# Attention feeding a maxout layer: the values' bound by one product with ones, and feed-forward products dealt out to beats by time

## The chip, the cores and the metric

The kernel runs on one core of one Trainium2 chip. The metric is the time of one execution on the device in microseconds (us); lower is better. A time is the median of several runs; a profile is one execution of its own, with a time of its own.

## The reference

Attention over 8 batches, 12 heads, 448 positions and 64 numbers a head, with queries and keys normalized first; its output, 3584 tokens of 768 numbers, goes through three 768 by 768 products whose elementwise maximum goes through a fourth. All inputs and the output are float32.

```
q_n, k_n = rmsnorm(q, g_q), rmsnorm(k, g_k)       # x / sqrt(mean(x*x) + 1e-6) * g
scores = matmul(q_n, k_n.T) / sqrt(64)
attn = exp(scores - max(scores)); attn = attn / (sum(attn) + 1e-9)
x = matmul(attn, v)                               # then [batch * seq, heads * dim]
h = maximum(maximum(x @ w1, x @ w2), x @ w3)
out = h @ w_out
```

## The kernel before, in words

**Precision.** A float32 operand is held as two float16 parts, an upper one and the rest, and a product is made of three float16 products (`TERMS`). So that the parts fit, operands are scaled by their largest magnitude. For the values of a batch that bound is made by `bound_v` (line 489) with `largest` (line 145): the largest of each partition is turned into one row by a product with the identity (`marks`, line 153), reduced on VectorE to one number (`top`, line 156), and spread to all partitions by a product with a row of ones (`most`, line 160). From it come `v_down` and `v_up` (lines 494 and 498). The bounds of the weights are made in the same way, through the same `largest`.

**The unit of attention** is a pair of heads `g`, 48 in all, six to a batch. The 448 queries of a pair are worked in four quarters, here called chunks. For a chunk, TensorE makes the scores (`sc`, line 541, 6 products), VectorE finds the row maxima (line 550), ScalarE takes the exponentials in place (`nm` line 558, line 567), VectorE the inverse of the sums (lines 636 and 640), ScalarE writes the upper half of the weights (`pp`, line 643), VectorE the lower half (line 653), and a transposing DMA turns them into `pt`. When all four are turned, TensorE multiplies them with the values (`av`, line 691, 24 products), and `xt` (lines 705 and 706) is one sixth of the feed-forward input of the batch. The first six pairs go another way (`PLAIN`), in float32. There are two buffers of scores: the scores of chunk k+1 go into the buffer of chunk k-1, and so wait for line 653 of chunk k-1.

**The unit of the feed-forward** is a generator that issues, at every step, three products; six steps make a block. `layer1` (line 715) makes a 128 by 448 block with 6 steps of three products of 448 columns; three blocks make one maximum (`hidden`, line 727). `layer2` (line 775) makes a 128 by 384 block of the output with 6 steps of three products of 384 columns; `result` (line 791) copies it scaled on ScalarE into `osb` (line 793), and `store` writes it out. A batch has 18 blocks of `layer1` (324 products) and 6 or, for odd batches, 8 blocks of `layer2` (108 or 144). All these blocks, and `marks` and `most`, take turns in three PSUM buffers (`ps_m`, tag "m").

**The order** is written by hand: each engine runs its instructions in the order in which the kernel issues them. A pair takes 12 beats (`beat(g, i)`, line 904). In a beat stand the attention steps due there (scores in beats 2, 5, 8 and 11, the values' product in beat 7), then `thirds(THIRDS[i])` steps of the feed-forward queue, then the works put off by `later(n, work)`, which are issued n beats later, at the end of that beat, by `tick`. `THIRDS` adds up to 25 steps a pair; one more is taken in beats 4 and 10 while two batches stand in the queue. A batch is put in the queue when its last pair is done, in beat 10 (beat 6 for the first). What is left of the last batch runs after the last pair, two steps a beat.

The chain of a step that ends a block: the next call of the generator puts the work that reads the block (`hidden` or `result`) off by one beat.

Of the kernel before, what the change touches and what calls it, by code (L numbers as in the profile page):

```python
# [9 lines left out]
F32 = mybir.dt.float32  # L10
# [6 lines left out]
P = 128  # L17
# [10 lines left out]
UP = 2.0 ** 14  # L28

LEAST = 2.0 ** -60  # L30
# [9 lines left out]
def qknorm_attention_maxout_ffn_kernel(  # L40
# [35 lines left out]
    nc = tc.nc  # L76
    B, H, S, D = q.shape
# [9 lines left out]
    HW = DO // NH  # L87
# [5 lines left out]
    const = ctx.enter_context(tc.tile_pool(name="const", bufs=1))  # L93
# [3 lines left out]
    ps_m = ctx.enter_context(tc.tile_pool(name="ps_m", bufs=3, space=bass.MemoryType.PSUM))  # L97
# [15 lines left out]
    def later(beats, work, last=False):  # L113

        due.setdefault(clock[0] + beats, ([], []))[last].append(work)
# [10 lines left out]
    make_identity(nc, ident)  # L126
    ones = const.tile([1, P], F32, name="ones")
    nc.vector.memset(ones, 1.0)
    warm = const.tile([P, 1], F32, name="warm")
    nc.vector.memset(warm, 0.0)  # L130
    nc.scalar.activation(warm, warm, AF.Exp)
# [13 lines left out]
    def largest(column, done, gaps):  # L145


        top = sb.tile([1, 1], F32, name="top", bufs=2)
        box = []

        def turn():
            box.append(ps_m.tile([P, 512], F32, name="marks", tag="m"))
            nc.tensor.matmul(box[0][0:1, 0:P], column, ident, start=True, stop=True)

        def reduce():
            nc.vector.tensor_reduce(top, box[0][0:1, 0:P], axis=AX, op=ALU.max)

        def spread():
            box.append(ps_m.tile([P, 512], F32, name="most", tag="m"))
            nc.tensor.matmul(box[1][:, 0:1], ones, top, start=True, stop=True)  # L160

        at = 0
        for gap, work in zip(gaps, (turn, reduce, spread, lambda: done(box[1][:, 0:1]))):
            at += gap
            later(at, work)
# [182 lines left out]
    def load_k(g):  # L348
        load_kv(g, "kr", k, 2, (nc.sync, nc.sync if g else nc.scalar))
# [130 lines left out]
    v_down = const.tile([P, B], F32, name="v_down")  # L480
# [8 lines left out]
    def bound_v(b):  # L489
        most = sb.tile([P, 1], F32, name="v_most", bufs=2)  # L490
        nc.vector.tensor_reduce(most, v_rows.pop(b), axis=AX, op=ALU.max)

        def scale(bound):
            nc.vector.tensor_scalar(
                out=v_down[:, b:b + 1], in0=bound, scalar1=LEAST, scalar2=1.0 / UP,
                op0=ALU.max, op1=ALU.mult,
            )
            nc.vector.reciprocal(v_up[:, b:b + 1], v_down[:, b:b + 1])

        largest(most, scale, (1, 2, 2, 2))  # L500


    def scale_v(g):
# [166 lines left out]
    def add_values(g):  # L670
        s = st[g]
        av = ps_a.tile([P, 512], F32, name="av", tag="a")
        s["av"] = av
        if g < PLAIN:
            vr, pt = s["vr"], pt_plain(s)
            for u in range(4):
                for h, half in enumerate(HALVES):
                    rows = half if u == 3 else slice(0, P)
                    group = 3 if u == 3 else 4 * h + u
                    nc.tensor.matmul(  # L680
                        av[half, :S], vr[rows, group], pt[rows, group],
                        start=u == 0, stop=u == 3,
                    )
            return
        vp, pt = s["vp"], s["pt"]
        for u in range(4):
            for n, (wp, vpart) in enumerate(TERMS):
                for h, half in enumerate(HALVES):
                    rows = half if u == 3 else slice(0, P)
                    group = 3 if u == 3 else 4 * h + u  # L690
                    nc.tensor.matmul(  # L691
                        av[half, :S], vp[rows, group, vpart], pt[rows, 7 * wp + group],
                        start=u == 0 and n == 0, stop=u == 3 and n == len(TERMS) - 1,
                    )
# [20 lines left out]
    def layer1(b, xs, hs, ft, j, keep):  # L715
        wt = w_sb[:, ft * NJ + j].rearrange("p a (c f) -> p a c f", c=NCT)
        acc = ps_m.tile([P, 512], F32, name="acc", tag="m")
        for c in range(NCT):
            for n, (wp, xp) in enumerate(TERMS):
                nc.tensor.matmul(  # L720
                    acc[:, :S], wt[:, wp, c], xs[c][:, xp],
                    start=(c == 0 and n == 0), stop=(c == NCT - 1 and n == 2),
                )
            yield
        later(1, lambda: hidden(b, acc, hs, ft, j, keep))

    def hidden(b, acc, hs, ft, j, keep):
        if j == 0:
            keep[ft] = sb.tile([P, S], F32, name="m", bufs=2)
            nc.scalar.copy(keep[ft], acc[:, :S])  # L730
            return
        m = keep[ft]
        most = m if j == 1 else acc[:, :S]
        nc.vector.tensor_tensor(out=most, in0=acc[:, :S], in1=m, op=ALU.max)
        if j == 2:
            ht = sb.tile([P, 2, S], F16, name="ht", bufs=6)
            hs.append(ht)

            def upper():
                nc.scalar.activation(ht[:, 0], most, AF.Copy, scale=H_DOWN)  # L740
                later(1, lower)

            def lower():
                nc.vector.scalar_tensor_tensor(  # L744
                    out=ht[:, 1], in0=most, scalar=H_DOWN, in1=ht[:, 0],
                    op0=ALU.mult, op1=ALU.subtract,
                )
                odd = (b % 2) * LEFT
                nc.gpsimd.tensor_copy(hx[:, ft, :, odd:odd + LEFT], ht[:, :, 3 * P:S])  # L749

            later(1, upper)


    def store(b, osb, row0, col0, n):
        tok = out[b * S:(b + 1) * S].rearrange("(p c) m -> c p m", c=NQ)
        while n:
            c, p0 = divmod(col0, QP)
            m = min(n, QP - p0)
            nc.sync.dma_start(out=tok[c, p0:p0 + m], in_=osb[row0:row0 + m])
            row0, col0, n = row0 + m, col0 + m, n - m  # L760
# [14 lines left out]
    def layer2(b, hs, tk, half, box):  # L775
        if half == 0:
            box[tk] = sb.tile([P, DO], F32, name="osb", tag="osb", bufs=3)
        osb = box[tk]
        acc = ps_m.tile([P, 512], F32, name="acc", tag="m")
        for f in range(NFT):  # L780
            assert f in split
            for n, (hp, wp) in enumerate(TERMS):
                lhs = hs[f][:, hp, tk * P:(tk + 1) * P] if tk < 3 else hx[:, f, hp]
                nc.tensor.matmul(  # L784
                    acc[:, :HW], lhs, wo_sb[:, f, wp, half * HW:(half + 1) * HW],
                    start=(f == 0 and n == 0), stop=(f == NFT - 1 and n == 2),
                )
            yield
        later(1, lambda: result(b, acc, osb, tk, half))

    def result(b, acc, osb, tk, half):
        by = o_scale[:, b:b + 1] if tk < 3 else o_pair[:, b // 2:b // 2 + 1]
        nc.scalar.activation(  # L793
            osb[:, half * HW:(half + 1) * HW], acc[:, :HW], AF.Copy, scale=by
        )
        if half == NH - 1:
            if tk < 3:
                later(2, lambda: store(b, osb, 0, tk * P, P))
            else:
                later(2, lambda: store(b - 1, osb, 0, 3 * P, LEFT))  # L800
                later(2, lambda: store(b, osb, LEFT, 3 * P, LEFT))
# [23 lines left out]
    queue = []  # L825
    decoded = [0]

    def thirds(n):
        while queue and n:
            try:  # L830
                next(queue[0])
                n -= 1
            except StopIteration:
                queue.pop(0)

    load_k(0)
    load_q(0)
# [2 lines left out]
    for i, src in enumerate((g_q, g_k)):  # L840
        nc.scalar.dma_start(
            out=gains[:, i], in_=src.rearrange("(o d) -> o d", o=1).broadcast_to([P, D])
# [53 lines left out]
    load_q(2)  # L896


    THIRDS = (2, 3, 2, 2, 3, 2, 2, 0, 2, 2, 3, 2)

# [1 line left out]
    def beat(g, i):  # L904
# [36 lines left out]
        if w >= 0 and i == (4 if w < PLAIN else 7):  # L941
            add_values(w)
        thirds(THIRDS[i] + (len(queue) > 1 and i % 6 == 4))
        if w >= 0 and i == (9 if w < PLAIN else 10):
            finish(w, x_of[w // NP])
# [35 lines left out]
        if g == 0 and i == 9:  # L981
            bound_v(0)
        if g > 1 and g % NP == 0 and g < G and i == 1:
            bound_v(g // NP)
# [28 lines left out]
    while queue or due:  # L1013
        thirds(2)
        tick()
# [32 lines left out]
```

## Time and profile before

| | |
|---|---|
| median of 3 runs | 1111.87 us (1109.64 to 1112.04) |
| the profiled execution, its own time | 1110.84 us |
| its span, first to last instruction | 1109.0 us |
| mean granted TensorE clock | 0.967 |
| busy: TensorE, ScalarE, VectorE, GpSimd | 92%, 70%, 68%, 63% of the span |
| first feed-forward product | 162.48 us |
| last product of attention (line 691) begins | 1013.33 us |

In the profile PE is TensorE's products, PEld its weight loads, DVE VectorE, ACT ScalarE, POOL GpSimd. A row of the timeline gives start, duration, engine, line, operation, output and inputs with their shapes, the count, and in brackets how long the engine sat idle before it and whom it waited for. The duration of a product is modelled and longer than its share of a dense row of products: what a product costs in such a row is read from the starts of what comes before and after, or from the chain, whose pieces do not overlap. A row of the waits gives who waited for whom, the sum, how often, and the longest.

### The profile page before, as it was taken

The numbers are of one execution on the slowest core, as the hardware profiler recorded it, in microseconds if no ns is written. First come the engines' busy times: TensorE is split into PE (matmuls) and PEld (weight loads), VectorE is DVE, ScalarE is ACT, GpSimd is POOL, SyncE is SP. The second block draws the span as 40 slices with busy tenths as digits, with TensorE's granted clock in tenths as the row PEclk, the third lists the DMA queues.
The fourth block names the chain that finished last, engine by engine and source line by source line (L and its number), as shares of the span: only waits on it lengthen the run. The fifth ranks groups of instructions, "written<-read, shape, count | busy, mean of one in ns | idle before, by whom it ended". The sixth has DMA issues, their size and how long they took to land. (4 is left out here: it accounts for less than half of the span.)

```text
span 1109.0 us, 18435 instructions
## 1 busy us (share of the span) xinstructions
PE 1017.1 (92%) x6184; PEld 500.3 (45%) x6184; DVE 755.3 (68%) x1397; ACT 771.2 (70%) x1767; POOL 702.4 (63%) x805
## 2 busy tenths in 40 slices
PE   4668759887899999999999999999999999999998
PEld 2334334343444444444444444444444444445554
DVE  4799988887667676776677766777677666662210
ACT  4599888767777687777777777777777777773001
POOL 5478888775767767677677675776767767610000
PEclk9697879998999999999999999999999999999999
DMA  5554567955888779777887798777877788564002
GB/s 150 161 164 151 139 175 142 188 118 102 172 147 147 134 153 179 152 142 139 170 149 143 143 164 173 144 137 154 169 142 139 140 173 154 91 106 87 1 1 57
DMA packets 426494, 152.30 MB, mean 137 GB/s; under 512 B 372896, under 2 KB 422048, under 8 KB 426400
## 3 DMA queue, kind: packets, MB, share of 16 engines
q1 hardware_dynamic: 425888, 150.95, 67.4%
q8 instruction: 49, 0.80, 0.3%
q14 instruction: 45, 0.37, 0.1%
q10 hardware_dynamic: 512, 0.18, 0.1%
HBM read 51.97 MB, written 11.01 MB: 57 GB/s over the span
## 5 line engine op out<-in xcount | busy, mean ns | idle before, releaser
L720 PE MATMUL acc<-xt,w_sb 128*128 128x448 f16 x2592 | 515.5, 354 | 2.7 <-DVE ht L744 2.2
L720 PEld LDWEIGHTS <-w_sb 128*128 128x128 f16 x2592 | 244.1, 98 | 260.8 <-issue 48.3
L550 DVE TENSOR_REDUCE sc<-sc 112x2 f32<-112x896 f32 x192 | 209.6, 1092 | 53.3 <-PE sc L541 52.2
L567 ACT ACTIVATE sc<-sc,nm,down 112x448 f32<-112x448 f32 x336 | 234.4, 698 | 11.2
L643 ACT ACTIVATE pp<-sc,rs 112x448 f16<-112x448 f32 x336 | 195.0, 633 | 52.0 <-ACT sc L567 47.4
L653 DVE SCALAR_TENSOR_TENSOR pp<-sc,rs,pp 112x448 f16<-112x448 f32 x336 | 212.9, 675 | 4.4 <-ACT pp L643 3.9
L784 PE MATMUL acc<-wo_sb,ht 128*128 128x384 f16 x864 | 151.9, 328 | 12.0 <-ACT osb L793 7.3
L558 ACT ACTIVATE nm<-sc,down 112x2 f32<-112x2 f32 x192 | 50.9, 265 | 158.2 <-DVE sc L550 157.7
L385 POOL TENSOR_TENSOR ri<-ri,half_neg 128x7 f32<-128x7 f32 x96 | 153.9, 1603 | 8.0
L541 PE MATMUL sc<-kt,qt 64*112 64x448 f16 x1008 | 132.1, 367 | 21.5 <-DVE pp L653 18.6
L749 POOL COPY hx<-ht 128x128 f16<-128x128 f16 x48 | 16.2, 337 | 168.0 <-DVE ht L744 167.6
L784 PEld LDWEIGHTS <-ht 128*128 128x128 f16 x864 | 81.4, 98 | 79.4 <-issue 29.0
L691 PE MATMUL av<-pt,vp 128*64 128x448 f16 x1008 | 109.9, 359 | 0.0
L541 PEld LDWEIGHTS <-qt 64*112 64x112 f16 x1008 | 54.2, 126 | 91.6 <-issue 52.4
L438 POOL TENSOR_TENSOR kp<-kn,kp 128x512 f16<-128x512 f32 x42 | 50.5, 1202 | 67.1 <-ACT kp L432 67.1
L636 DVE TENSOR_SCALAR rs<-sc 112x2 f32<-112x2 f32 x168 | 26.7, 159 | 91.1 <-ACT sc L567 91.0
L519 POOL TENSOR_TENSOR vp<-vr,vp 128x448 f16<-128x448 f32 x42 | 44.5, 1059 | 63.0 <-ACT vp L513 61.3
L691 PEld LDWEIGHTS <-vp 128*64 128x64 f16 x1008 | 50.1, 109 | 54.7 <-issue 29.5
L706 DVE SCALAR_TENSOR_TENSOR xt<-av,xt 128x448 f16<-128x448 f32 x42 | 26.2, 625 | 67.0 <-ACT xt L705 67.0
L370 DVE TENSOR_REDUCE ss<-sq 128x7 f32<-128x448 f32 x96 | 61.0, 637 | 10.4 <-ACT sq L361 6.4
L438 POOL TENSOR_TENSOR qp<-qn,qp 112x512 f16<-112x512 f32 x42 | 48.6, 1156 | 19.2 <-ACT qp L432 19.2
L505 POOL TENSOR_SCALAR vr<-vr,v_up 128x448 f32<-128x448 f32 x42 | 60.4, 1438 | 0.0
(111 smaller groups left out, 1202.6 us busy)
## 6 DMA issues: line engine op xcount, KB each, us to landing
raw<-in_moe_w_dram SPq DMA_DIRECT2D x18, 768.0 KB, 4.3
qr<-in_q_dram SPq DMA_DIRECT2D x48, 224.0 KB, 2.8
vr<-in_v_dram SPq DMA_DIRECT2D x96, 96.0 KB, 2.5
kr<-in_k_dram SPq DMA_DIRECT2D x95, 96.0 KB, 3.0
raw<-in_moe_w_out_dram SPq DMA_DIRECT2D x6, 768.0 KB, 5.1
pt<-pp SPq DMA_TRANSPOSE x168, 4.0
out_dram<-osb SPq DMA_DIRECT2D x8, 336.0 KB, 3.0
out_dram<-osb SPq DMA_DIRECT2D x8, 288.0 KB, 3.6
```

Of the source, the lines that this page charges most:

```text
L370: nc.vector.tensor_reduce(sums[g % 2][:sq.shape[0], KQ[what]], sq, axis=AX, op=ALU.add)
L385: nc.gpsimd.tensor_tensor(out=ri, in0=ri, in1=half_neg[:, at], op=ALU.pow)
L438: nc.gpsimd.tensor_tensor(out=parts[:, 1], in0=n, in1=parts[:, 0], op=ALU.subtract)
L505: nc.gpsimd.tensor_scalar(out=vr, in0=vr, scalar1=v_up[:, g // NP:g // NP + 1], scalar2=None, op0=ALU.mult,)
L541: nc.tensor.matmul(sc[:QP, h, :S], qt[rows, qp, c], kt[rows, kp, KEYS[h]], start=n == 0, stop=n == len(TERMS) - 1,)
L550: nc.vector.tensor_reduce(sc[:QP, 0, S + 8:S + 10], sc[:QP, :, :S], axis=AX, op=ALU.max, negate=True)
L567: nc.scalar.activation(to, sc[:QP, h, :S], AF.Exp, bias=nm[:, h:h + 1], scale=down[:QP], accum_out=total,)
L643: nc.scalar.activation(pp[:, 0, h], sc[:QP, h, :S], AF.Copy, scale=rs[:, h:h + 1])
L653: nc.vector.scalar_tensor_tensor(out=pp[:, 1, h], in0=sc[:QP, h, :S], scalar=rs[:, h:h + 1], in1=pp[:, 0, h], op0=ALU.mult, op1=ALU.subtract,)
L691: nc.tensor.matmul(av[half, :S], vp[rows, group, vpart], pt[rows, 7 * wp + group], start=u == 0 and n == 0, stop=u == 3 and n == len(TERMS ...
L720: nc.tensor.matmul(acc[:, :S], wt[:, wp, c], xs[c][:, xp], start=(c == 0 and n == 0), stop=(c == NCT - 1 and n == 2),)
L784: nc.tensor.matmul(acc[:, :HW], lhs, wo_sb[:, f, wp, half * HW:(half + 1) * HW], start=(f == 0 and n == 0), stop=(f == NFT - 1 and n == 2),)
```

## The change

Four edits:

1. `bound_v` no longer calls `largest`. It makes one product of a 128 by 128 matrix of ones (one column of ones, read again and again) with the column of the partitions' largest (`spread`, put off by two beats), so that every partition gets their sum. That sum stands in place of the largest as the bound; `v_down` and `v_up` follow one beat later. The bounds of the weights stay as they were.
2. A step of `layer1` counts 1.0 and a step of `layer2` counts 384/448, and `thirds` keeps what is owed from beat to beat: it issues steps while half a step or more is owed.
3. `THIRDS` has a 2 where it had its second 3 (beat 4), so that a pair is given 24.
4. `result` is put off by no beat: it is issued in the beat in which the next step finds the block ended.

```
+    ones_c = const.tile([P, 1], F32, name="ones_c")
+    nc.vector.memset(ones_c, 1.0)
...
-        def scale(bound):
+        box = []
+
+
+        def spread():
+            box.append(ps_m.tile([P, 512], F32, name="most", tag="m"))
+            nc.tensor.matmul(
+                box[0][:, 0:1], ones_c.broadcast_to([P, P]), most, start=True, stop=True
+            )
+
+        def scale():
             nc.vector.tensor_scalar(
-                out=v_down[:, b:b + 1], in0=bound, scalar1=LEAST, scalar2=1.0 / UP,
+                out=v_down[:, b:b + 1], in0=box[0][:, 0:1], scalar1=LEAST, scalar2=1.0 / UP,
                 op0=ALU.max, op1=ALU.mult,
             )
             nc.vector.reciprocal(v_up[:, b:b + 1], v_down[:, b:b + 1])
 
-        largest(most, scale, (1, 2, 2, 2))
+        later(2, spread)
+        later(3, scale)
...
-            yield
+            yield 1.0
         later(1, lambda: hidden(b, acc, hs, ft, j, keep))
...
-            yield
-        later(1, lambda: result(b, acc, osb, tk, half))
+            yield HW / S
+        later(0, lambda: result(b, acc, osb, tk, half))
...
+    owed = [0.0]
+
     def thirds(n):
-        while queue and n:
+        owed[0] += n
+        while queue and owed[0] >= 0.5:
             try:
-                next(queue[0])
-                n -= 1
+                owed[0] -= next(queue[0])
             except StopIteration:
                 queue.pop(0)
+        if not queue:
+            owed[0] = 0.0
...
-    THIRDS = (2, 3, 2, 2, 3, 2, 2, 0, 2, 2, 3, 2)
+    THIRDS = (2, 3, 2, 2, 2, 2, 2, 0, 2, 2, 3, 2)
```

What this moves, read from the order of the built programs. On PE, in the second layer of batch 1, where the bound of batch 3 is made, there stood before (`acc` are the blocks, `ht` the second layer's input, `vp` the values):

```order
L784 MATMUL acc_4372<-wo_sb_95,ht_3444 128x384
L153 MATMUL marks_4382<-ident_72,v_most_4359 1x128
L784 LDWEIGHTS ht_3629
...
L784 MATMUL acc_4413<-wo_sb_95,ht_3956 128x384
L160 MATMUL most_4462<-top_4361,ones_77 128x1
L691 LDWEIGHTS vp_4312
```

and now:

```order
L796 MATMUL acc_4371<-wo_sb_97,ht_3613 128x384
L500 MATMUL most_4384<-v_most_4343,ones_c_79 128x1
L796 LDWEIGHTS ht_3819
...
L796 MATMUL acc_4413<-wo_sb_97,ht_3819 128x384
L703 LDWEIGHTS vp_4292
```

One product and one PSUM buffer are left of two, at about the place of the first; the second, ahead of the values' product, is gone.

On ACT, in the second layer of batch 2, from the exponentials of chunk 0 of a pair (`sc_5799`) to the upper half of chunk 1, there stood before:

```order
L567 ACTIVATE sc_5799<-sc_5799,nm_5819,down_128 112x448 x2
L432 CAST kp_5831<-kn1_89 128x512
L793 ACTIVATE osb_5673<-acc_5674,o_scale_103 128x384
L793 ACTIVATE osb_5673<-acc_5753,o_scale_103 128x384
L643 ACTIVATE pp_5846<-sc_5799,rs_5843 112x448 x2
L432 CAST qp_5858<-qn_5777 112x512
L558 ACTIVATE nm_5887<-sc_5865,down_128 112x2
L567 ACTIVATE sc_5865<-sc_5865,nm_5887,down_128 112x448 x2
L793 ACTIVATE osb_5809<-acc_5810,o_scale_103 128x384
L643 ACTIVATE pp_5906<-sc_5865,rs_5903 112x448 x2
```

and now:

```order
L579 ACTIVATE sc_5774<-sc_5774,nm_5794,down_130 112x448 x2
L434 CAST kp_5811<-kn1_91 128x512
L805 ACTIVATE osb_5719<-acc_5720,o_scale_105 128x384
L805 ACTIVATE osb_5719<-acc_5761,o_scale_105 128x384
L655 ACTIVATE pp_5826<-sc_5774,rs_5823 112x448 x2
L434 CAST qp_5838<-qn_5745 112x512
L570 ACTIVATE nm_5863<-sc_5844,down_130 112x2
L579 ACTIVATE sc_5844<-sc_5844,nm_5863,down_130 112x448 x2
L805 ACTIVATE osb_5806<-acc_5807,o_scale_105 128x384
L655 ACTIVATE pp_5888<-sc_5844,rs_5885 112x448 x2
```

These copies stand where they stood: the second layer of this batch begins later by some products, and its copies follow their blocks sooner by a beat. The last copy of the same batch moves. Before, from the exponentials of the pair's last chunk on:

```order
L643 ACTIVATE pp_6044<-sc_6000,rs_6041 112x448 x2
L705 ACTIVATE xt_6056<-av_5971 128x448
L513 CAST vp_6072<-vr_4439 128x7x64
L558 ACTIVATE nm_6077<-sc_6058,down_128 112x2
L567 ACTIVATE sc_6058<-sc_6058,nm_6077,down_128 112x448 x2
L432 CAST kp_6089<-kn0_88 128x512
L793 ACTIVATE osb_5915<-acc_6010,o_scale_103 128x384
```

and now:

```order
L655 ACTIVATE pp_6023<-sc_5981,rs_6020 112x448 x2
L717 ACTIVATE xt_6038<-av_5952 128x448
L525 CAST vp_6054<-vr_4423 128x7x64
L805 ACTIVATE osb_5911<-acc_6006,o_scale_105 128x384
L570 ACTIVATE nm_6060<-sc_6040,down_130 112x2
L579 ACTIVATE sc_6040<-sc_6040,nm_6060,down_130 112x448 x2
```

The copy went from behind the next chunk's exponentials to ahead of them.

Between two values' products there now stand 72 products of the first layer or 84 of the second, where 75 of either stood. In the first layer the products between one scores group and the next are 21, 21, 18 and 12 with the values' product, where they were 21, 21, 21 and 12: the third stretch, from the scores of beat 2 to those of beat 5, lost three. In the second layer they are 24, 24, 21 and 15. Both programs have one place where the queue is empty, between the end of batch 0's second layer and the start of batch 1: two scores groups stand there side by side. After the last pair both run the whole of batch 7.

## Prediction

> **What bounds the kernel now.** I read the page first, for its span and the engines' totals.
>
> ```profile
> span 1109.0 us, 18435 instructions
> PE 1017.1 (92%) x6184; PEld 500.3 (45%) x6184; DVE 755.3 (68%) x1397; ACT 771.2 (70%) x1767; POOL 702.4 (63%) x805
> ```
>
> TensorE is the fullest, but its busy time is modelled and does not say how much of the span it loses. The chain of waits does, near the end of the attention:
>
> ```profile
> 918.46 2.51 PE av L691 x24
> 920.96 0.70 PE sc L541 x6
> 921.67 4.08 PE acc L720 x21
> ...
> 938.39 2.51 PE av L691 x24
> ...
> 1001.11 12.29 PE acc L784 x75
> ```
>
> From one values' product to the next there are 19.93 us. A first-layer product costs 4.08/21 = 0.194 us, so 75 make 14.57; four scores groups make 2.8 and the values 2.51: 19.9 together. In the first layer TensorE never rests. A second-layer product costs 12.29/75 = 0.164 us, so the same count of 75 is 12.3, and such a pair would last 17.6 us. The two layers were dealt out evenly by count and not by time. So the question is where TensorE waits; I asked for its waits alone by stages. From 307 us to 1002 us, 35 pairs, there are two kinds:
>
> ```profile
> PE acc L784 <- ACT osb L793: 7.3, 7, 1.3
> PE sc L541 <- DVE pp L653: 5.1, 14, 0.9
> ```
>
> Together 12.4 us. Ahead of that, between 182 and 262 us, where the feed-forward weights are still being prepared, its waits are of these kinds above all:
>
> ```profile
> PE sc L541 <- DVE pp L653: 5.3, 5, 1.7
> PE acc L720 <- DVE ht L744: 2.2, 3, 1.7
> ```
>
> and between 262 and 298 us, where the second layer of batch 0 finds its weights not ready:
>
> ```profile
> PE acc L784 <- DVE wo_sb L310: 3.4, 3, 2.2
> PE most L160 <- DVE top L156: 1.3, 1, 1.3
> PE acc L784 <- ACT wo_sb L305: 1.2, 2, 0.8
> ```
>
> Last, the timeline of PE, DVE and ACT through the second layer of batch 2, where the change does its work:
>
> ```profile
> 525.86 3.59 PE L784 MATMUL acc<-wo_sb,ht 128*128 128x384 f16 x21
> 530.04 0.78 PE L541 MATMUL sc<-kt,qt 64*112 64x448 f16 x6 [0.59 <-DVE pp L653]
> 531.11 1.06 ACT L793 ACTIVATE osb<-acc,o_scale 128x384 f32<-128x384 f32 x2
> 531.76 1.14 PE L784 MATMUL acc<-wo_sb,ht 128*128 128x384 f16 x6 [0.94 <-ACT osb L793]
> 532.82 0.38 PE L153 MATMUL marks<-ident,v_most 128*1 128x128 f32 x2
> 533.13 2.12 PE L784 MATMUL acc<-wo_sb,ht 128*128 128x384 f16 x12
> 533.26 1.28 DVE L653 SCALAR_TENSOR_TENSOR pp<-sc,rs,pp 112x448 f16<-112x448 f32 x2 [0.59 <-ACT pp L643]
> 535.40 0.58 ACT L793 ACTIVATE osb<-acc,o_scale 128x384 f32<-128x384 f32 x1
> 536.03 0.65 PE L784 MATMUL acc<-wo_sb,ht 128*128 128x384 f16 x3 [0.78 <-ACT osb L793]
> 539.37 0.38 PE L160 MATMUL most<-top,ones 1*128 1x1 f32 x2
> 539.68 2.58 PE L691 MATMUL av<-pt,vp 128*64 128x448 f16 x24
> ```
>
> TensorE comes 0.59, 0.94 and 0.78 us early here, 2.31 us in all: once for a scores buffer, twice for one of the three PSUM buffers, of which `marks` and `most` take one each.
>
> **The change part by part.** The sum is made against the profiled execution's own 1110.84 us, 1.03 us under the median of the runs.
>
> *One product with ones.* `marks` starts at 532.82 and what follows it at 533.13, so it costs 0.31 us of TensorE, and it goes eight times. Batches 0 and 1 have theirs in the starting stage, ahead of waits that swallow it: 0. Batches 2 to 7 have theirs between 293 us and the end, in dense work: 6 x 0.31 = 1.9 us. The product that stays also takes 0.31 us (539.37 to 539.68); it now loads 128 full rows where it loaded one. These rows bound what that may add:
>
> ```profile
> L461 PE MATMUL rows<-ident,kn 128*128 128x128 f32 x24 | 6.0, 401 | 4.4 <-POOL kn L421 3.1 <-DVE kn L421 0.7 <-DVE w_most L257 0.6
> L160 PE MATMUL most<-top,ones 1*128 1x1 f32 x30 | 5.8, 261 | 1.4 <-DVE top L156 1.3
> ```
>
> A full float32 product of 128 columns lasts 0.14 us more than `most`, so the new one adds 0 to 0.8 us over six; with one column streamed it is nearest the second row, and I take 0. [...] The two small VectorE steps that go were off the path, except once (1.3 us, counted below). The new wait of VectorE for `most` (line 505 after) has behind it the lower halves that free the scores; `most` is due one beat earlier on PE, so I take 0.
>
> *Dealing by time, 307 to 1002 us.* A second-layer pair now has 84 products: 84 x 0.164 = 13.8 us, against 72 x 0.194 = 14.0 in the first. In the even batch shown, everything on ACT and DVE after the scores that ended at 525.86 is one chain, whose later links do not hang on TensorE: the lower halves end at 533.26 + 1.28 = 534.54, 8.68 us later, and the third copy at 535.98, 10.12 later. TensorE, with its new 24 products, scores, 15 + 6 products and one `most`, asks for the next scores buffer after 3.94 + 0.70 + 3.44 + 0.31 = 8.39 us, 0.3 early, and for the third copy's buffer after another 0.70 + 3 x 0.164, 0.3 early. So 0.6 of 2.3 us stay; there are two such batches after 307 us, 1.2 us left. The three odd batches share what the total leaves, (12.4 - 4.6)/3 = 2.6 us each. Of that I let one wait stand, at the passage from the first layer to the second:
>
> ```profile
> 396.08 0.77 PE L541 MATMUL sc<-kt,qt 64*112 64x448 f16 x6 [0.31 <-DVE pp L653]
> ```
>
> Here 3 first-layer and 18 second-layer products stood ahead, 0.58 + 2.95 us, and by the order 15 and 3 will, 2.91 + 0.49: 0.13 us less, so the wait becomes 0.44, with rounding 0.5, three times: 1.5 us.
>
> In the first layer nothing waits now, but one stretch of four loses three products, 0.58 us. What slack it had is read from the end of the lower halves to the scores that need them. The shortest that this stretch has in a first-layer pair is here:
>
> ```profile
> 454.21 1.26 DVE L653 SCALAR_TENSOR_TENSOR pp<-sc,rs,pp 112x448 f16<-112x448 f32 x2
> 455.84 0.78 PE L541 MATMUL sc<-kt,qt 64*112 64x448 f16 x6
> ```
>
> 455.84 - 455.47 = 0.37 us, so this one would wait 0.21, and the others less or not at all. The feed-forward steps will fall on other beats, so I take 1 us for all 28 first-layer pairs; if each waited 0.2, it would be 5.6. Left over: 1.2 + 1.5 + 1.0 = 3.7 of 12.4 us, a gain of 8.7; the ends are 12.4 (all goes) and 12.4 - 2.7 - 5.6 = 4.1.
>
> *Dealing by time, 182 to 307 us.* Here the first layer stretches into the next pair: 12 products (2.3 us) move from pairs that wait anyway for VectorE to ahead of the second layer. What leaves is earned only where TensorE did not wait, 0 to 2.3 us. What arrives stands before the waits for `wo_sb` (3.4 + 1.2) and is hidden by them; and a scores group that stood behind 18 second-layer products now stands behind 6. I take 2 us of the 4.6 there, and the 1.3 us before `most`, less 0.3 for the products moved: 3 us. The ends are a loss of 2.3 (nothing earned, all paid) and a gain of 8 (4.6 + 1.3, and 2 us of clock, next).
>
> The clock bears on this stage. The windows show it granted at half after TensorE had little to do, and at 0.59 right after the wait for `top`:
>
> ```profile
> 268.00:270.00 2.00, 0.28 (x1) 0.00 (x0) 2.00 (x4) 1.93 (x6) 0.00 (x0) 0.50 0.03 10
> 296.00:298.00 2.00, 0.70 (x8) 0.37 (x6) 1.00 (x4) 1.49 (x6) 1.92 (x3) 1.00 1.05 184
> 298.00:300.00 2.00, 2.00 (x14) 1.03 (x16) 2.00 (x4) 1.87 (x5) 1.92 (x3) 0.59 1.02 204
> ```
> ```profile
> 297.92 4.21 PE L691 MATMUL av<-pt,vp 128*64 128x448 f16 x24
> ```
>
> The values' product took 4.21 us there and 2.58 at 539.68, 1.6 more. If the wait of 1.3 us brought the slow clock on, removing it earns 1.6 more; I leave that to the range, since the queue is empty in these beats either way. [...]
>
> *Copies in their own beat.* By the order the copies of a batch mostly stand where they stood among the exponentials, and the last one a softmax earlier. No time of its own; its risk is a rival. *The tail* from 1019 us runs the same 324 + 144 products; the 24 products now ahead of it (3.9 us) cover the making of `xt` as 21 did: 0.
>
> Sum: 1.9 + 8.7 + 3 = 13.6 us off, 1110.84 - 13.6 = 1097.2; by the median 1098.3. I say 1097. The ends: 1.9 + 12.4 + 8 = 22.3 off, 1088.5; and 1.9 - 0.8 + 4.1 - 2.3 = 2.9 off, 1107.9.
>
> **The rivals.** *The wait moves and half the gain with it.* ScalarE has little to spare in a second-layer pair, and some stretches of the first layer have no slack to speak of:
>
> ```profile
> 392.00:412.00 20.00, 18.94 (x129) 10.00 (x128) 14.96 (x33) 15.54 (x37) 14.29 (x18) 1.00 0.73 150
> ```
> ```profile
> 330.20 1.27 DVE L653 SCALAR_TENSOR_TENSOR pp<-sc,rs,pp 112x448 f16<-112x448 f32 x2
> 331.57 0.78 PE L541 MATMUL sc<-kt,qt 64*112 64x448 f16 x6
> ```
>
> 15.54 us of 20 are ScalarE's there, and the second view leaves 0.10 us between the lower halves and the scores. If first-layer pairs wait 0.2 us each and the starting stage gives nothing: 1.9 + 4.1 = 6 off, 1105. Against it: TensorE has 13.8 - 12.3 = 1.5 us more to do in each second-layer pair than before, and the stretch with 0.10 keeps its length.
>
> *Slower: ScalarE stands before a block that is not ended.* ScalarE takes its instructions in order, so a copy issued a beat sooner, if its last product is not done, holds the upper halves behind it, VectorE's lower halves behind those, and the scores that need the buffer. Before 1019 us there are 48 copies; a hold of one step, 3 x 0.164 = 0.49 us each, passed on in full, is 23.5 us, so 1097.2 + 23.5 = 1121. From 13.6/48 = 0.28 us a copy on it eats the gain. Against it: all of ScalarE's waits between 182 and 1002 us begin with
>
> ```profile
> ACT nm L558 <- DVE sc L550: 140.9, 128, 2.8
> ```
>
> and none is for a product of line 784; and ScalarE reaches the copies shown 5 us and more after the scores, when TensorE has passed their blocks. [...]
>
> *More than forecast*: the starting stage keeps its clock and loses its waits, 8 us there: 1.9 + 8.7 + 8, 1092. *The change does not do what it says*: the steps owed round to the same counts, 1110. The order shows 72 and 84, so this is nearly out.
>
> **How the numbers follow.** Forecast 0.64, half the gain 0.18, more 0.09, slower 0.06, no effect 0.03. A difference of 0.2%, 2.2 us, is about what a measurement of this kernel can tell. Forecast, half and more are all faster: 0.91; same 0.03; slower 0.06. The range takes in the ends of the sum, 1088 to 1107: it leaves out the slower case, no effect and a little of the rest.
>
> **What would show it.** In the profile after: TensorE's waits from about 300 us to the last scores under 5 us, with `osb` nearly gone from them and what is left at `sc` behind line 665; values' products 19.3 to 19.7 us apart in both layers; no line 153 for `v_most`; the tail still some 85 us. Wrong would be ScalarE waiting for line 796 before the tail, a first-layer pair with waits at every third scores group, or a stage up to 307 us longer than now.

## The result and the profile after

The changed kernel takes 1099.66 us (median of 4 runs, 1097.75 to 1103.31), beside 1111.95 us for the kernel before on the same chip: a ratio of 0.9896, 95% interval 0.9881 to 0.9911. The forecast was 1097.0 us, 1088 to 1107. The profiled execution took 1099.43 us. Its page has this span and these engines:

```profile
span 1097.6 us, 18387 instructions
PE 1011.4 (92%) x6168; PEld 499.4 (45%) x6168; DVE 755.7 (69%) x1390; ACT 771.8 (70%) x1767; POOL 704.2 (64%) x805
```

The span is 11.4 us shorter. These are TensorE's waits from 302 to 990 us, with three figures each: microseconds in all, times, longest.

```profile
PE sc L553 <- DVE pp L665: 5.7, 13, 1.3
PE acc L796 <- DVE ht L756: 0.5, 2, 0.3
```

The waits for `osb` (7.3 us before) are gone; the waits for a scores buffer have not become fewer (5.1 before). In the timeline, the second layer of batch 2, which the prediction showed with 2.31 us of waits, has 0.26 left, for a hidden row:

```profile
519.99 1.66 PE L796 MATMUL acc<-wo_sb,ht 128*128 128x384 f16 x8
521.90 2.77 PE L796 MATMUL acc<-wo_sb,ht 128*128 128x384 f16 x16 [0.26 <-DVE ht L756]
524.61 0.78 PE L553 MATMUL sc<-kt,qt 64*112 64x448 f16 x6
525.15 1.06 ACT L805 ACTIVATE osb<-acc,o_scale 128x384 f32<-128x384 f32 x2
525.32 2.61 PE L796 MATMUL acc<-wo_sb,ht 128*128 128x384 f16 x15
527.76 0.28 PE L500 MATMUL most<-v_most,ones_c 128*128 128x1 f32 x2
527.90 1.14 PE L796 MATMUL acc<-wo_sb,ht 128*128 128x384 f16 x6
```

What is left at the scores sits in the first layer and at its passage to the second, always at the scores of beat 5, where the stretch ends that lost three products: seven waits of 0.17 to 0.18 us, three of 0.25 and three of 1.25. Here is one of the last, with the rows of ScalarE and VectorE between those of TensorE:

```profile
366.69 0.78 PE L553 MATMUL sc<-kt,qt 64*112 64x448 f16 x6
367.23 1.16 ACT L655 ACTIVATE pp<-sc,rs 112x448 f16<-112x448 f32 x2
368.27 0.62 ACT L434 CAST qp<-qn 112x512 f16<-112x512 f32 x1
368.78 0.55 ACT L752 ACTIVATE ht<-acc 128x448 f16<-128x448 f32 x1
369.37 0.62 DVE L756 SCALAR_TENSOR_TENSOR ht<-acc,ht 128x448 f16<-128x448 f32 x1 [1.71 <-ACT ht L752]
369.91 1.09 DVE L562 TENSOR_REDUCE sc<-sc 112x2 f32<-112x896 f32 x1
370.91 1.27 DVE L665 SCALAR_TENSOR_TENSOR pp<-sc,rs,pp 112x448 f16<-112x448 f32 x2
372.23 0.78 PE L553 MATMUL sc<-kt,qt 64*112 64x448 f16 x6 [1.25 <-DVE pp L665]
```

VectorE stands 1.71 us for ScalarE's upper half of a hidden row, with the row maximum (line 562) and the lower halves (line 665) behind it, though the scores for that maximum were done at 367.47. TensorE pays 1.25 of it.

That is the change as a whole. It has three parts, and the prediction gave each a price; the experiments take them apart.

### The profile page after: what moved, and what is told of

Same layout as the page of the kernel before. It is cut to its first block, busy times and chain, and to the rows that moved or that the text cites. A ratio compares the mean times of both kernels' runs of the same rounds, so it can differ in the third digit from the quotient of the medians.

```text
span 1097.6 us, 18387 instructions
## 1 busy us (share of the span) xinstructions
PE 1011.4 (92%) x6168; PEld 499.4 (45%) x6168; DVE 755.7 (69%) x1390; ACT 771.8 (70%) x1767; POOL 704.2 (64%) x805
## 5 line engine op out<-in xcount | busy, mean ns | idle before, releaser
L440 POOL TENSOR_TENSOR qp<-qn,qp 112x512 f16<-112x512 f32 x42 | 49.2, 1173 | 19.8 <-ACT qp L434 19.8
```

Of the source, the lines that this page charges most:

```text
L440: nc.gpsimd.tensor_tensor(out=parts[:, 1], in0=n, in1=parts[:, 0], op=ALU.subtract)
```

## The experiments

To see where a kernel gains, I read three points of TensorE's timeline in every profiled execution: the first feed-forward product (162.48 us before), the start of batch 1's first layer (306.56) and the start of the tail's first layer (1019.27). What lies ahead of the first scatters from 159.9 to 164.4 whatever is edited, and what lies behind the last is 89.7 to 89.9 us in all kernels; the change acts between. The last column is the stage from batch 1 to the tail less TensorE's busy time in it, so its waits. The ratios are to the kernel before on the same chip.

Two things in these stages are chance, since each row has one execution. The first few microseconds of batch 1 ran at half clock in some executions (last section): the granted clock over its first 8 us was 1.00 with the copies alone and with copies and dealing, 0.87 before, 0.90 with the old table, and 0.73 to 0.84 in the others. So the last column but one counts from the 101st feed-forward product of batch 1 on, where all run at full clock, except that the old table has two more stretches of 3.41 us at half. And the kernel of the last row runs the same instructions in the same order up to batch 1 as the two rows of the short stretch, but took 142.9 us there beside 140.0 twice: a difference of under 3 us in that column says little.

| kernel | median us | ratio, 95% interval | first product to batch 1 | batch 1 to tail | from its 101st product to tail | waits from batch 1 to tail |
|---|---|---|---|---|---|---|
| before | 1111.95 | 1 | 144.1 | 712.7 | 686.2 | 12.5 |
| product alone | 1109.94 | 0.9987, 0.9978–0.9995 | 144.2 | 712.0 | 684.9 | 13.9 |
| copies alone | 1103.58 | 0.9925, 0.9912–0.9938 | 141.8 | 705.4 | 679.3 | 6.8 |
| dealing alone | 1108.08 | 0.9967, 0.9954–0.9980 | 139.0 | 713.8 | 686.6 | 11.7 |
| product and copies | 1101.44 | 0.9903, 0.9888–0.9919 | 143.2 | 703.7 | 677.0 | 6.9 |
| product and dealing | 1102.41 | 0.9920, 0.9905–0.9935 | 139.9 | 709.3 | 681.8 | 9.9 |
| copies and dealing | 1102.91 | 0.9925, 0.9913–0.9937 | 139.5 | 707.9 | 681.7 | 8.3 |
| all three, the change | 1099.66 | 0.9896, 0.9881–0.9911 | 140.0 | 705.5 | 678.2 | 7.1 |
| the change again | 1098.67 | 0.9885, 0.9871–0.9898 | 139.9 | 705.3 | 678.1 | 7.1 |
| the change, old table | 1105.57 | 0.9950, 0.9936–0.9963 | 145.1 | 707.6 | 681.3 | 7.7 |
| short at the values | 1095.41 | 0.9855, 0.9841–0.9869 | 140.0 | 701.3 | 674.0 | 3.7 |
| short at the values again | 1096.22 | 0.9856, 0.9838–0.9874 | 140.0 | 700.4 | 673.7 | 3.5 |
| and all hidden rows later | 1098.73 | 0.9881, 0.9865–0.9896 | 140.6 | 702.2 | 674.4 | 4.0 |
| and three hidden rows later | 1094.52 | 0.9847, 0.9830–0.9864 | 142.9 | 699.3 | 671.7 | 1.6 |

**The product alone.** The change with its other two parts undone.

```diff
-            yield HW / S
-        later(0, lambda: result(b, acc, osb, tk, half))
+            yield 1.0
+        later(1, lambda: result(b, acc, osb, tk, half))
...
-    THIRDS = (2, 3, 2, 2, 2, 2, 2, 0, 2, 2, 3, 2)
+    THIRDS = (2, 3, 2, 2, 3, 2, 2, 0, 2, 2, 3, 2)
```

> The change's one product with ones alone; steps dealt by count from the old table, copies a beat later, as before the change. If the product's saving is earned in full, 6 x 0.48 = 2.9 us in dense work and up to 2.9 us in the starting stage (1.3 of wait for the largest value, 1.6 of slow clock after it): 1106 to 1109. By the prediction's term 1.9 + 1.3: 1108.7. If TensorE waits for copies and scores in those second layers all the same, so that the saving only lengthens other waits: 1111.

Measured: 1109.94 us, 1.2 us less than before beside it (1111.13), between the first case and the third. Two of TensorE's waits from 302 to 990 us:

```profile
PE acc L796 <- DVE v_down L505: 6.6, 5, 1.5
...
PE acc L796 <- ACT osb L805: 1.9, 2, 0.9
```

The waits for `osb` fell from 7.3 to 1.9, but 6.6 us of a new kind took their place: the product's result holds one of the three PSUM buffers until VectorE reads it, and VectorE reads it late. The first of the five, in the timeline:

```profile
413.25 0.28 PE L500 MATMUL most<-v_most,ones_c 128*128 128x1 f32 x2
413.33 1.28 DVE L665 SCALAR_TENSOR_TENSOR pp<-sc,rs,pp 112x448 f16<-112x448 f32 x2
415.86 0.14 DVE L505 TENSOR_SCALAR v_down<-most 128x1 f32<-128x1 f32 x1
416.05 0.65 PE L796 MATMUL acc<-wo_sb,ht 128*128 128x384 f16 x3 [1.53 <-DVE v_down L505]
```

By itself the shorter way to the bound is worth little here, since TensorE stands at the same ring of buffers anyway.

**The copies alone.** One character of the kernel before.

```diff
-        later(1, lambda: result(b, acc, osb, tk, half))
+        later(0, lambda: result(b, acc, osb, tk, half))
```

> The kernel before with its copies of the second layer issued one beat sooner, nothing else. If the copies alone take the waits for osb away (7.3 us of 12.4 before the change), TensorE comes that much sooner and some of it turns into waits for scores: 1105 to 1109. If the dealing by time is needed for it, because the copies stand behind the exponentials that TensorE's early scores wait for anyway: 1110 to 1112. If a copy then holds ScalarE ahead of an unended block: over 1113, with ScalarE behind line 784 in the trace.

Measured: 1103.58 us, 7.7 us less than before beside it (1111.27), more than any of the three cases gave. TensorE's waits from 302 to 990 us are now two kinds, and the second is a single one just ahead of batch 1 (2.4 us before the change as well):

```profile
PE sc L541 <- DVE pp L653: 6.6, 15, 0.9
PE sc L541 <- ACT sc L567: 2.8, 1, 2.8
```

The second layer of batch 2 in its timeline:

```profile
521.95 0.78 PE L541 MATMUL sc<-kt,qt 64*112 64x448 f16 x6
522.65 3.59 PE L784 MATMUL acc<-wo_sb,ht 128*128 128x384 f16 x21
524.26 1.08 ACT L793 ACTIVATE osb<-acc,o_scale 128x384 f32<-128x384 f32 x2
526.82 0.78 PE L541 MATMUL sc<-kt,qt 64*112 64x448 f16 x6 [0.58 <-DVE pp L653]
527.52 1.15 PE L784 MATMUL acc<-wo_sb,ht 128*128 128x384 f16 x6
...
538.44 0.58 ACT L793 ACTIVATE osb<-acc,o_scale 128x384 f32<-128x384 f32 x1 [0.94 <-PE acc L784]
```

All 7.3 us at `osb` are gone. Before, the first two copies started 531.11 - 525.15 = 5.96 us after the scores, behind a whole softmax; here 524.26 - 521.95 = 2.31 us after them and ahead of it, and TensorE finds the buffer free. The stage is 7.3 us shorter; that this is what those waits had been is in part chance, for its waits fell by 5.6 us only (12.5 to 6.8), and the rest is modelled busy time, some 1 us of it because batch 1 began at full clock here, where the kernel before had 2.05 us of it at half. From the 101st product on, the copies bring 7.0 us. The third case shows itself too, on a small scale: ScalarE stands five times for a block that is not ended, 0.94 us in the last row and 4.7 in all, and the waits at the scores grow from 5.1 to 6.6 us.

**The dealing alone, and with each of the other parts.** For the dealing alone both other parts are undone; in the two runs behind it, one of them.

```diff
-        later(2, spread)
-        later(3, scale)
+        largest(most, scale, (1, 2, 2, 2))
...
-        later(0, lambda: result(b, acc, osb, tk, half))
+        later(1, lambda: result(b, acc, osb, tk, half))
```

> The dealing by time alone: count by time and the new table, with the two products for the values' bound and the copies a beat late, as before the change. From the runs with two parts each, if the parts simply give way to one another: without the earlier copies the waits for osb come back, more than the 2.5 us that they were with the one product, since marks and most take a buffer each: 1105 to 1108. If the dealing takes the waits away by itself, as the prediction has it: 1101 to 1103.

> The change with its copies of the second layer issued one beat later again. By the prediction the earlier beat has no time of its own: 1099 to 1101. If the earlier copy is what took the waits for osb away (7.3 us before the change, none after), they come back in part: 1103 to 1107, with rows of TensorE behind line 805.

> The change without its product with ones: the two products and the two VectorE steps of before stay. If the product earned 2.9 us in dense work and 2.9 in the starting stage: 1102.6 to 1105.5, with a values' product of about 4.2 us near 298 us again. If the dealing alone hides it: 1099.7, and the product is worth nothing in company.

Measured: the dealing alone 1108.08 us, just past the end of the first case and far from what my forecast made of it; with the product 1102.41, between its two cases; with the copies 1102.91, in its first, though its values' product near 298 us took 2.58 us and not 4.2. The dealing alone has from 302 to 990 us, among others,

```profile
PE sc L543 <- DVE pp L655: 5.8, 13, 1.3
...
PE acc L786 <- ACT osb L795: 2.5, 6, 0.6
PE marks L155 <- ACT osb L795: 1.9, 2, 0.9
```

that is, 4.4 us behind copies. Its waits from batch 1 to the tail fall by only 0.7 us (12.5 to 11.7), and the stage is 1.1 longer: the same products (1944 and 756 of the two layers) cost TensorE 1.8 us more of modelled busy time (700.2 to 702.1). Some 0.7 of that is the clock, half for 3.4 us at the start of batch 1 and for 2.05 in the kernel before; from the 101st product on the stage is 0.4 longer and no more. The rest I put down, without a run that shows it, to the places where the scores cut the products. What the dealing alone gains lies ahead of batch 1: 5.1 us. Beside the product it does help behind it: 709.3 us against 712.0 for the product alone, and the 6.6 us of waits for `v_down` are gone. In the change with late copies, 2.5 us of waits for `osb` come back:

```profile
PE acc L796 <- ACT osb L805: 2.5, 5, 0.9
```

and its stage of 709.3 us against 705.5 puts the earlier copy at 3.8 us in company (3.6 from the 101st product on). Without the product the stage is 707.9, which puts the product at 2.4; but that execution had the full clock at the start of batch 1, and from the 101st product on it is 3.6.

**Everything but the dealing.**

```diff
-            yield HW / S
+            yield 1.0
-    THIRDS = (2, 3, 2, 2, 2, 2, 2, 0, 2, 2, 3, 2)
+    THIRDS = (2, 3, 2, 2, 3, 2, 2, 0, 2, 2, 3, 2)
```

> The change without its dealing: one product with ones, copies in their own beat, but steps counted as before and 25 a pair. The copies alone gave 7.7 us. If the product adds its 3 us, the dealing is worth under 2 us in the whole: 1100 to 1101.5. If TensorE waits for VectorE's reading of the product (line 505) as it did with the product alone (6.6 us), the product adds nothing: 1103 to 1104.

Measured: 1101.44 us, in the first case. The wait for `v_down` is not there; from 302 to 990 us TensorE waits for the scores buffer, before batch 1, and for nothing else.

```profile
PE sc L553 <- DVE pp L665: 6.9, 16, 0.9
PE sc L553 <- ACT sc L579: 2.4, 1, 2.4
```

So beside both other parts the dealing brings 3.2 us ahead of batch 1 (143.2 to 140.0), hardly more than that column scatters, and costs 1.8 behind it (703.7 to 705.5; 1.2 from the 101st product on). The two ratios, 0.9903 and 0.9896, do not tell the kernels with and without it apart.

**The change with the old table**, 25 steps a pair, still counted by time.

> The change with the old table, 25 steps a pair in place of 24, still counted by time. First-layer pairs then last 19.94 us again without waits. If the evenness is what earns, an even batch, which has 139 steps of a first-layer step's time for the 150 that the table asks for, runs out 11 steps (6.4 us) ahead of its end, and TensorE waits there for scores; some 3 to 4.5 us each in batches 2 and 4 and in batch 0, against the 5 us of first-layer waits saved: 1102 to 1107. If only the count in the second layer matters: 1095 to 1099.

Measured: 1105.57 us, in the first case. Its main row shows the queue run out: once ahead of batch 1, and twice more at the end of an even batch (all between 302 and 990 us):

```profile
PE sc L553 <- ACT sc L579: 8.1, 3, 2.9
```

The new table with steps counted one by one, the other half of the dealing, was not run by itself.

**The short stretch moved to the values' product.** Beat 4 gets its third step back, beat 6 gives one.

```diff
-    THIRDS = (2, 3, 2, 2, 2, 2, 2, 0, 2, 2, 3, 2)
+    THIRDS = (2, 3, 2, 2, 3, 2, 1, 0, 2, 2, 3, 2)
```

> The three products that the table gave up are put back in beat 4 and taken from beat 6, so that the stretch with the values' product is the short one. If the waits that are left in the first layer (4.95 us after the change: 3 of 1.25, 7 of 0.18 and passages) come from the stretch of beats 2 to 5 having 18 products, 3.49 us, where the others last 4.1 and more, they go: 4 to 5 us less than the changed kernel, 1095, and TensorE's waits behind line 665 between 302 and 990 us fall from 5.7 to under 1.5 us. If instead VectorE's stand for the hidden rows (ht) makes them, wherever TensorE's steps lie, the scores one stretch later wait as long: 1099 to 1100.

> The short stretch at the values' product alone, again, beside the others on this chip: 1094 to 1096.5, some 3.5 to 4.5 us less than the changed kernel.

Measured: 1095.41 us, and 1096.22 on another chip. The wait at the scores from 302 to 990 us:

```profile
PE sc L553 <- DVE pp L665: 2.3, 4, 0.7
```

5.7 us became 2.3, not quite the 1.5 that I had named, and the stage is 4.1 and 5.0 us shorter. From the 101st product on it is 4.2 and 4.5. The small waits were the stretch's length; of each 1.25 the stretch had made 0.5, and 0.7 stayed.

**The 0.7 us that stayed: VectorE standing for the hidden row.** With the stretch moved, line 756 is issued a beat later wherever it would stand ahead of a row maximum; in a second kernel only ahead of the maximum of beat 3 (`% 12` for `% 3`, and without the exception).

```diff
-                later(1, lower)
+                later(2 if clock[0] % 3 == 1 and ft < NFT - 1 else 1, lower)
```

> The short stretch at the values' product as in the first experiment, and the lower half of the hidden rows (line 756) issued a beat later where it would stand ahead of a row maximum (not for the last of six). If the wait left there (0.7 us, once in two batches, 2.3 us at scores in all from 302 to 990 us) is VectorE standing for ScalarE's upper half with the maximum behind it, it goes: 1 to 2 us less than the first experiment, 1093 to 1094.5, and pairs of 19.4 us throughout the first layer. If the accumulator that is held a beat longer is then waited for: rows of TensorE's acc behind line 756, and 1096 or more.

> The short stretch at the values' product, and the lower half of the hidden rows a beat later only where it would fall ahead of the maximum of beat 3 (three times in the program). If the accumulators held longer made the waits of the run that delayed all of them (six of 0.44 us, 0.6 with what hangs on them), these three cost none: the three pairs of 20.13 us become 19.4, 2.2 us less than the kernel with the short stretch alone beside it, about 1093.

Measured: 1098.73 us for all of them, a miss. From 302 to 990 us no wait at the scores is left, but the rival's row stands there:

```profile
PE acc L732 <- DVE ht L756: 2.6, 6, 0.4
```

The accumulators held a beat longer are waited for. That is 2.6 us for 2.3, so the trace has the stage at 702.2 against 701.3; why the median lies 2.5 to 3.3 us above those of the kernel without this edit, taken on other chips, the trace does not show. The second kernel moves three rows and no more, and took 1094.52 us:

```profile
PE sc L553 <- DVE pp L665: 0.2, 1, 0.2
```

So the 1.25 us is shown from two sides: 18 products in the stretch, and the order on VectorE. Against 1096.22 for the moved stretch alone on the same chip, the intervals (0.9830 to 0.9864, 0.9838 to 0.9874) show no difference; from batch 1 to the tail it is 1.2 and 2.1 us shorter than the two executions of that kernel, and from the 101st product on 2.0 and 2.4, where 2.2 were expected. What is sure is the moved stretch: beside the change's two ratios, 0.9896 and 0.9885, it has 0.9855 and 0.9856.

## Why the prediction was right, and where it was not

Time and sign came out right, 11.4 us off the span where 13.6 were forecast. But two terms of the sum were given to the wrong part, and that these errors nearly cancelled was luck.

- *One product with ones, -1.9.* From batch 1 to the tail, where five of the six stand, it brings 0.7 us by itself and 2.4 in company, from the 101st product on 1.3 and 3.6. It costs less than the 0.31 us taken for it, to which the prediction let it add 0 to 0.8 us in six: 527.90 - 527.76 = 0.14. So 0.31 + 0.31 - 0.14 = 0.48 is saved each time, 2.9 in six. What the sum had at 0, VectorE's reading of `most`, is a wait of 6.6 us in the kernel with this part alone, and none in the whole.
- *Dealing by time, 307 to 1002 us, -8.7.* **This step failed.** The dealing alone lengthens that stage by 1.1 us, and added to the other two parts by 1.8; added to the copies it lengthens it by 2.5, and only added to the product does it shorten it, by 2.7. The 12.4 us of waits did fall to 6.2, but of the kind that fell, `osb`, the dealing alone leaves 4.4 of 7.3 us behind copies, and the copies alone leave none.
- *Copies in their own beat, "No time of its own".* **This is the same failure seen from the other side.** Alone they bring 7.3 us in that stage (7.0 from the 101st product on) and 7.7 in the time; in company 3.8. I had read the order of the whole change against that of before. There dealing lets a block end later and the sooner copy makes up for it, so that the copies "mostly stand where they stood": true of both edits together, and of neither by itself. By the order in the traces, of the 36 copies of batches 1 to 5, 28 go ahead of an exponential or an upper half with the copies alone, and 25 fall behind one with the dealing alone; with both, 28 stand where they stood, 5 earlier and 3 later.
- *Left over, 3.7 of 12.4.* It was 6.2. The first layer was put at 1.0 with an end at 5.6, and measured 3 x 1.25 + 7 x 0.17 = 4.9. The 0.21 us that the shortest slack gave was near (0.17 to 0.18), but came seven times; and that "the feed-forward steps will fall on other beats", which was named and not priced, put a hidden row ahead of a maximum three times. The two even batches, put at 1.2, have 0.5 for hidden rows; the passage has 0.25 us three times, not 0.5.
- *182 to 307 us, -3.* From the first feed-forward product to batch 1 it was -4.1, and here the dealing does earn most of it: 5.1 us alone, against a scatter of up to 3, which the copies' 2.3 do not clear; the product brings nothing. The waits for `wo_sb` (4.6 us) went as reckoned, but between 262 us and batch 1 the waits for scores behind the lower halves grew by 4.3 (0.6 to 4.9), where the sum had allowed 2.6. The slow clock behind the wait for `top` is not settled (last section).
- *The tail, 0.* 89.7 us before and after.
- *The rivals.* Of half the gain, the short waits in first-layer pairs were there, at 4.9 us instead of 5.6; that the starting stage gives nothing was not. The slower case has its mechanism, too: with the copies alone ScalarE stands five times for an unended block, 4.7 us in all. With the dealing it has none from 310 to 985 us, neither in the change nor in the kernel with copies and dealing; with product and copies five are left, 1.4 us in all. So the dealing does something for the copies there that the prediction did not see. That ScalarE runs in order, on which this rival rests, is seen in the kernel before: from 529.14 to 535.96 us its rows come as the built program has them, the copies at 531.11 us ahead of the upper half at 532.05.
- *The signs.* The waits were to be under 5 us and were 6.2; the values' products were to be 19.3 to 19.7 us apart in both layers, and from batch 1 to the last scores they are 19.3 to 19.8 except for five pairs of 20.2 and 20.7.

Right in the whole, the prediction would have been wrong on each part by itself: it would have kept the dealing for the middle of the program, where it earned something only beside the product without the earlier copies, and called the copies idle.

## What to carry to other kernels

When an engine waits for a ring of PSUM buffers, look first at where the reader of the result is queued on its own engine: here one beat sooner for a copy was worth more (7.7 us) than an even load for TensorE (3.4). Where edits overlap, price each against the kernel before by itself, since an order read off the whole change cannot say which edit moved a row and which moved it back. When a table has to give up work, take it from the stretch whose closing scores have the most slack; here the place of three products was worth some 4 us.

## What the hardware showed unexpectedly

The load of 128 full rows went beside running products; that of one row did not. In the change the load for the product with ones:

```profile
527.60 0.35 PEld L500 LDWEIGHTS most<-v_most,ones_c 128*128 128x128 f32 x2
```

It starts 0.16 us ahead of its product, while line 796's products run, and the product then takes 0.14 us of its own. The `most` of before, with its one row, took 0.31 us in place (539.37 to 539.68), and its load began with it, at 539.37. But the load of `marks`, 128 rows of one column, also began only with its product, at 532.82, so that the rows are the cause is not shown.

The granted clock did not follow the length of a rest. In the kernel with the copies alone, 1.09 us of rest at the place where before had 1.30 left the values' product at 2.58 us, where before had 4.21:

```profile
297.58 0.35 PE L160 MATMUL most<-top,ones 1*128 1x1 f32 x2 [1.09 <-DVE top L156]
297.86 2.58 PE L691 MATMUL av<-pt,vp 128*64 128x448 f16 x24
```

That alone could be a threshold between the two. But ahead of batch 1, the scores after a rest of 2.81 us ran at full speed in the kernel without the product, and after 2.92 us at half of it in the changed kernel, 0.78 against 1.37 us:

```profile
302.16 0.78 PE L543 MATMUL sc<-kt,qt 64*112 64x448 f16 x6 [2.81 <-ACT sc L569]
```
```profile
301.16 1.37 PE L553 MATMUL sc<-kt,qt 64*112 64x448 f16 x6 [2.92 <-ACT sc L579]
```

A rest of 1.30 us with half a clock behind it and one of 2.81 with the full one are no matter of length alone.

The traces show more. In the clock records of the kernel before and of the changed one the half-clock stretches from 150 us to the tail begin on one grid of steps of 3.41 us and last one step or two: before at 161.84, 267.65, 298.37 and 305.20 us, which is 31, 9 and 2 steps apart, after at 159.36, 268.58 and 299.31, 32 and 9 apart. Where the grid lies differs even between two executions of the changed kernel: ahead of batch 1 the clock fell at 299.31 us in one and at 303.22 in the other, where the scores at 302.19, after the same rest of 2.92 us, took 0.78 us. These are two steps of the grid in the changed kernel, then two in the kernel without the product; behind the step's length stands TensorE's busy time, and the third number from the end is the granted clock:

```profile
295.89:299.30 3.41, 1.27 (x12) 0.37 (x8) 2.64 (x6) 2.70 (x8) 3.18 (x6) 1.00 0.59 125
299.30:302.72 3.42, 1.56 (x7) 0.67 (x8) 2.26 (x6) 2.88 (x8) 3.33 (x3) 0.50 1.06 228
```
```profile
297.61:301.03 3.42, 1.73 (x16) 0.56 (x12) 2.58 (x8) 2.87 (x7) 3.26 (x6) 1.00 0.72 148
301.03:304.44 3.41, 2.28 (x15) 1.21 (x16) 1.88 (x5) 2.87 (x8) 3.33 (x4) 1.00 1.06 232
```

After a step in which TensorE was busy for 1.27 us the clock fell, after one of 1.73 it did not. In the profiled executions of the kernel before and of the changed one, from 140 us to 10 us before the end, it fell after all six full-clock steps with a busy share under 0.42, and after none of the 527 with 0.53 or more; of the seven between it fell after one, with 0.52. So what goes with a fall here is how little TensorE did in a fixed step, not how long one rest was. Busy time is modelled, and no run changed that share alone, so the bounds are rough.
